# Loading one input block earlier, regrouping three small copies, and swapping the last two matmul groups in a hand-ordered state-space and MLP kernel

## Chip, cores and metric

The kernel runs on one core of a Trainium2 chip. The metric is the device time of one execution in microseconds (us). A core has five engines that run their own instruction lists side by side and wait for each other by semaphores: TensorE (PE, matmuls into psum), VectorE (DVE), ScalarE (ACT), GpSimd (POOL) and SyncE (SP, which here only issues DMAs).

## What is computed

The input x has 2048 rows of 448 columns. It is normalized per row (xn), and two branches work on xn: a linear state-space recurrence over the rows, and an MLP behind a second normalization. The result is their gated product added to x. Cut to what matters:

```python
def _A_ref(x, ...):                       # state-space branch, 448 complex states
    Lam_bar = jnp.exp(dt * Lam)
    B_bar = ((Lam_bar - 1.0) / Lam)[:, None] * Bmat
    Bu = jnp.einsum("bld,pd->blp", x + 0j, B_bar)
    for t in range(L):                    # L = 2048
        h = Lam_bar[None, :] * h + Bu[:, t, :]
    return 2.0 * jnp.einsum("blp,dp->bld", hseq, Cmat).real + x * Dskip

def _B_ref(x, w1, b1, w2, b2):            # MLP, 448 -> 1792 -> 448
    h = _gelu(jnp.einsum("bsd,df->bsf", _layernorm(x), w1) + b1)
    return jnp.einsum("bsf,fd->bsd", h, w2) + b2

xn = _layernorm(x)
return x + _A_ref(xn, ...) * _silu(_B_ref(xn, ...))
```

## The kernel before

**Tiling.** The 2048 rows are eight blocks of 256 (x0 to x7). A block is two "parities" of 128 rows each, even rows and odd rows, because the recurrence is done two rows at a time. Two blocks make a group; there are four groups, g = 0 to 3. Matrices are kept with 128 partitions; 448 columns are 3 x 128 + 64, so w1 is stored as four slices of rows, of which the fourth (w1's last 64 rows and, as a 65th, the bias b1) fills only half of the partitions.

**Stages of a group.** Normalize (bn_stats L381, bn_aggr L385, then a reciprocal root, on POOL as L424 to L428, then the scaling, L450 on DVE or L451 on ACT), giving xn and xn2 (normalized twice); transpose both (DMA transposes, L89; for the first block PE transposes instead). Then

- `mm1`: xn2 times w1, then gelu. For group 0 in halves (`mm1_half`, matmuls L746, gelu L752), one block at a time; for the other groups with all 512 columns (L726, gelu L736). L726 uses the partition halves in two steps, `own` and `other`, and for this needs w1's last 64 rows a second time, in partitions 64 to 127 of the fourth slice. A unit of `mm1` covers two of the 14 column tiles of w1 and writes two psum banks; units go round the bank pairs (0,1), (2,3), (5,6).
- `mm2`: gelu's output times w2 (14 matmuls L760), plus b2 (DVE, L763, reads bank 5 or 6), silu (ACT, L764).
- `bu`: xn times the input matrix (L652, bank 4), copied out by ACT (L656); `ssm`: the scan over rows on DVE (L677) with its rotations before and after.
- `ym`: the states times the output matrices (L795, L798, L801), then on DVE the gate (L810) and the sum with x (L813, on DVE or POOL), then the store. `skip` (L776 on DVE, L775 on POOL) prepares the term with Dskip; in the last block it makes three steps, so that x + Dskip term times the gate is ready in `xr`.

**The second copy of w1's last rows.** Lines L848 to L854 make four copies, W0 to W3, one for each load chunk of w1 (512, 512, 512 and 256 columns). Each may run on ACT (L851) or DVE (L852). Every unit of `mm1` after group 0 (L726) waits for all four, because they write under one name, `w1b`; for the same reason each copy waits for the one before it.

**The last block.** Where the last `ym` (group 3, block 1) handles odd rows, it is split by columns into two parts, 0 to 256 and 256 to 448 (L824), each with its own psum bank, gate, sum and store; the even rows have one part of 448 columns. The store of the 256 columns is issued from ACT, the other two from SP (L822).

**Preparing the matrices.** While group 0 is in work, DVE and ACT build the recurrence's input matrix: `combine` multiplies one half (L590 on ACT or L591 on DVE, into one of two `tmp` buffers) and adds the other (L593 on DVE). Its seven results LB0 to LB6 are transposed by DMA into BT0 to BT6 for `bu`.

**The order.** All work is first recorded as tasks (a few instructions of one engine each, with what they read and write), in the order in which the Python code comes to them. `Plan.link` works out who depends on whom. Then `emit` writes the tasks out in the order of one long hand-kept list, `ORDER` (L161 to L180): an entry is a task's number or its name (W0 to W3, H.. for the first half of an `mm1` unit, D.., O.., B..). Each engine gets its tasks in that order and runs them strictly one after another; a task waits by semaphore for its dependencies on other engines and, where there is one, on its own. A second list, `SECOND` (L181 to L183), names tasks that take the other of two allowed engines. There is no scheduler at run time, and no code outside of the two lists decides the order.

Of the kernel before, what the change touches and what calls it, by code (L numbers as in the profile page):

```python
# [9 lines left out]
BF = dt.bfloat16  # L10
# [148 lines left out]


ORDER = [int(k) if k.isdigit() else k for k in """  # L161
ST 0 18 22 10 88 1 19 16 23 15 20 2 21 11 3 9 27 12 24 8 17 14 13 25 5 7 6 26 89 4 28 90 96 91 29 45 30 97 92 98 93 31 46 47 94 99 48 63 103
95 32 53 100 49 54 101 50 102 33 51 52 114 64 44 106 65 55 38 108 116 56 105 115 39 107 57 109 40 117 58 118 41 120 42 119 36 110 122 34 121
111 37 144 124 35 104 123 43 60 112 62 125 59 B0 126 DH 72 113 67 B1 296 68 69 128 B2 70 127 300 298 73 B3 151 130 129 299 191 148 132 303
131 149 297 134 133 301 302 150 304 136 152 135 142 155 138 66 156 143 153 140 154 137 157 271 139 71 146 308 305 74 165 76 75 141 306 61
309 145 79 307 166 268 82 272 163 BF 83 77 310 86 169 164 181 158 277 269 159 401 180 400 270 170 167 398 147 160 274 W0 405 168 404 W1 182
W2 399 W3 171 280 402 403 183 161 406 172 H10 173 275 162 H11 192 278 184 281 356 174 H12 175 357 185 358 311 78 410 360 80 176 81 H13 361
312 411 229 407 412 408 362 230 409 501 502 H15 363 500 314 188 231 359 315 504 383 189 506 503 H16 232 505 507 508 H14 186 368 178 364 369
187 233 509 365 179 512 366 234 H21 513 177 237 316 H20 367 238 460 313 239 458 510 461 235 242 190 246 373 243 459 245 514 195 193 196 511
236 247 H24 244 H23 194 199 251 466 85 197 200 84 464 198 203 87 249 252 201 253 240 202 241 205 248 204 317 370 206 215 262 217 207 382 318  # L170
218 257 216 258 319 208 254 259 250 D0 263 255 260 209 320 371 256 264 321 210 219 221 D1 220 211 223 265 266 273 222 376 267 413 374 322
224 212 225 D2 326 276 213 227 226 379 325 279 228 214 D3 327 282 331 465 333 323 283 414 285 375 377 332 380 H26 415 334 467 H22 O00 335
470 324 484 462 471 328 289 330 284 416 339 329 286 340 463 261 341 342 H30 290 343 344 417 337 336 292 515 548 418 O01 345 H25 351 516 346
549 H31 485 347 287 348 468 288 293 349 H33 350 550 372 352 338 554 419 378 353 518 354 294 384 291 420 295 421 469 385 387 422 551 423 517
O10 555 388 574 391 389 424 519 428 386 427 475 392 429 437 394 435 425 520 472 426 390 430 436 431 521 432 476 473 481 522 438 O11 433 381
523 440 395 482 447 393 478 434 448 524 575 439 441 442 443 449 450 453 444 451 445 525 446 355 479 452 H32 526 454 H34 455 552 396 556 553
456 397 529 457 H36 557 H35 530 560 531 558 561 539 527 538 559 486 565 483 474 528 487 536 477 535 489 480 534 532 562 537 541 O20 566 533
540 493 488 542 563 544 567 490 564 568 491 494 492 543 545 496 569 546 571 570 O21 495 547 581 572 497 573 578 498 576 O30 499 577 582 593
579 585 583 594 595 580 596 589 584 586 587 590 588 591 592
""".split()]  # L180
SECOND = [int(k) if k.isdigit() else k for k in """  # L181
142 143 144 157 163 167 171 173 195 201 219 223 308 309 407 411 413 416 484 485 508 509 512 515 516 518 519 575 W0 W1 W2
""".split()]  # L183


# [743 lines left out]
```

## Time and profile before

| what | value |
|---|---|
| median of three runs | 155.3 us (155.3 to 155.35) |
| the profiled execution's own time | 155.38 us |
| its span, first to last instruction | 153.6 us |
| granted TensorE clock | 0.997 |
| busy share of PE, DVE, ACT, POOL | 97%, 80%, 72%, 22% |
| HBM read, written | 6.20 MB, 1.84 MB |

How to read the profile's rows. A row of the timeline gives the start in us from the beginning of the span, the duration in us, the engine, the line of the kernel, the operation, the tile that it writes and those that it reads (numbers left out, so that w1_sb and w2_sb both read `w_sb`, and xn_sb and xn2_sb both `xn_sb`), the shape, and how many instructions were merged into the row; in brackets stands how long the engine stood idle before it and what ended that. PEld is PE's loading of weights, which runs beside its matmuls; SPq and ACTq are the issuing of DMAs by these engines. The ends of matmuls are modelled. Instructions of DVE and ACT overlap a little: one that waits for nothing starts somewhat before the end of the one before it. A row of the DMA view gives the tile, the issuing engine, how many DMAs, their size, and the us from issue to landing.

### The profile page before, as it was taken

How to read it: one execution, taken by the hardware profiler on the slowest of the kernel's cores; microseconds unless marked ns; L12 is line 12 of the kernel's file. 1: busy time of each engine (PE TensorE's matmuls, PEld its weight loads, DVE VectorE, ACT ScalarE, POOL GpSimd, SP SyncE). 2: the span in 40 equal slices, each digit the busy share in tenths (PEclk: the TensorE clock that was granted, in tenths of full speed). 3: DMA queues.
4: the chain of work that ended last, by engine and by line, in shares of the span. 5: the costliest groups of instructions: out<-in, count | busy, mean ns of one | idle time of the engine just before them, and what ended most of it. 6: DMA issues, size and time to landing. Idle time of an engine off the chain costs nothing.

```text
span 153.6 us, 2968 instructions
## 1 busy us (share of the span) xinstructions
PE 148.8 (97%) x1055; PEld 88.1 (57%) x1055; DVE 122.8 (80%) x263; ACT 110.8 (72%) x190; POOL 34.2 (22%) x114
## 2 busy tenths in 40 slices
PE   7999999999999999999999999999999999999991
PEld 2689955445564555665544456755666455555560
DVE  5686989998967999899898864494986972999564
ACT  3867769899959988699999999832294889661100
POOL 6466491074000050310003310210006000000230
PEclk9999999999999999999999999999999999999998
DMA  4999976989996870000020121121300100001013
GB/s 94 282 316 399 263 178 125 154 157 179 223 141 110 153 137 0 0 4 0 2 46 18 38 82 64 21 38 27 94 4 0 60 0 0 4 0 62 0 66 113
DMA packets 31512, 14.04 MB, mean 91 GB/s; under 512 B 25733, under 2 KB 31113, under 8 KB 31498
## 3 DMA queue, kind: packets, MB, share of 16 engines
q1 hardware_dynamic: 31344, 13.79, 39.5%
q8 instruction: 8, 0.13, 0.3%
q10 hardware_dynamic: 154, 0.07, 0.2%
q14 instruction: 6, 0.05, 0.1%
HBM read 6.20 MB, written 1.84 MB: 52 GB/s over the span
## 4 chain that ended last, share of the span: by engine, by line
PE 80%; ACT 5%; DVE 4%; DMA 3%; POOL 3%; SPq 2%; issue 1%; ACTq 0%; DVEq 0%
PE psum L726 22%; PE psum L760 21%; PE psum L652 14%; PE psum L795 13%; PE psum L798 4%; DMA w_sb<-in_B_w_dram 3%; PE psum L631 3%; PE psum L746 2%; SPq L90 2%; ACT xn_sb L451 1%; DVE lnst L381 1%; POOL lnw L426 1%; ACT WT L574 1%; PE psum L801 1%; ACT L576 1%
## 5 line engine op out<-in xcount | busy, mean ns | idle before, releaser
L760 PE MATMUL psum<-w_sb,gT 128*128 128x448 bf16 x224 | 44.5, 353 | 0.0
L726 PE MATMUL psum<-xn2T,w_sb 64*128 64x512 bf16 x294 | 33.7, 378 | 0.2 <-ACT w_sb L851 0.2
L760 PEld LDWEIGHTS psum<-w_sb,gT 128*128 128x128 bf16 x224 | 21.8, 98 | 19.5 <-issue 0.2
L736 ACT ACTIVATE gT<-psum,b1f 128x512 bf16<-128x512 f32 x42 | 25.9, 690 | 3.2 <-PE psum L726 3.1
L726 PEld LDWEIGHTS psum<-xn2T,w_sb 64*128 64x128 bf16 x294 | 15.6, 109 | 16.8 <-issue 2.3
L652 PE MATMUL psum<-xnT,BT 128*128 128x256 bf16 x196 | 24.1, 273 | 0.0
L652 PEld LDWEIGHTS psum<-xnT,BT 128*128 128x128 bf16 x196 | 18.5, 98 | 6.4 <-issue 3.1
L677 DVE TENSOR_TENSOR_SCAN s_f<-cw,cur,v_sb 128x256 f32<-128x256 f32 x21 | 15.1, 740 | 0.2
L451 ACT ACTIVATE xn_sb<-x_all,lnw 128x448 bf16<-128x448 bf16 (+1 forms) x21 | 13.4, 668 | 1.3 <-POOL lnw L428 1.2
L764 ACT ACTIVATE g_sb<-o 128x448 bf16<-128x448 f32 x16 | 8.9, 572 | 6.4 <-DVE o L763 6.2
L746 PE MATMUL psum<-xn2T,w_sb 128*128 128x256 bf16 x112 | 12.9, 273 | 0.4 <-issue 0.3
L746 PEld LDWEIGHTS psum<-xn2T,w_sb 128*128 128x128 bf16 x112 | 11.8, 111 | 1.2 <-issue 0.6
L795 PE MATMUL psum<-CZ,h_sb 128*128 128x448 bf16 x56 | 11.9, 353 | 0.0
L810 DVE TENSOR_TENSOR t<-psum,g_sb 128x448 bf16<-128x448 f32 (+2 forms) x10 | 5.7, 575 | 7.4 <-ACT g_sb L764 3.7
L656 ACT ACTIVATE u_sb<-psum 128x512 bf16<-128x512 f32 x12 | 7.1, 593 | 5.8 <-PE psum L652 5.8
L763 DVE TENSOR_TENSOR o<-psum,b2bc 128x448 f32<-128x448 f32 x16 | 9.6, 613 | 1.5 <-PE psum L760 1.5
L795 PE MATMUL psum<-CQ,h_sb 128*128 128x448 bf16 (+2 forms) x54 | 10.6, 332 | 0.0
L752 ACT ACTIVATE gT<-psum 128x512 bf16<-128x512 f32 x14 | 8.2, 590 | 3.3 <-PE psum L746 3.2
L381 DVE BATCH_NORM_STATS2 lnst<-x_all 128x6 f32<-128x448 bf16 x14 | 8.3, 612 | 1.2 <-DMA x_all<-in_A_x_dram 1.1
L590 ACT ACTIVATE tmp<-Cr,cw 128x448 f32<-128x448 bf16 (+1 forms) x12 | 7.9, 672 | 1.0 <-DVE CQ L593 0.9
L691 POOL TENSOR_TENSOR cwk<-s_f,ang 128x3 f32<-128x3 f32 x3 | 1.1, 352 | 32.6 <-DVE s_f L677 32.5
L795 PEld LDWEIGHTS psum<-CZ,h_sb 128*128 128x128 bf16 x56 | 5.4, 98 | 4.7 <-issue 0.4
(156 smaller groups left out, 211.9 us busy)
## 6 DMA issues: line engine op xcount, KB each, us to landing
out_dram<-tmp SPq DMA_DIRECT2D x7, 224.0 KB, 2.0
x_all<-in_A_x_dram SPq DMA_DIRECT2D x3, 448.0 KB, 4.7
w_sb<-in_B_w_dram SPq DMA_DIRECT2D x3, 448.0 KB, 7.0
w_sb<-in_B_w_dram SPq DMA_DIRECT2D x3, 384.0 KB, 5.2
Bn<-in_A_B_im_dram SPq DMA_DIRECT2D x1, 336.0 KB, 9.1
Bn<-in_A_B_re_dram SPq DMA_DIRECT2D x1, 336.0 KB, 9.6
x_all<-in_A_x_dram SPq DMA_DIRECT2D x2, 112.0 KB, 2.1
x_all<-in_A_x_dram SPq DMA_DIRECT2D x1, 224.0 KB, 4.4
```

Of the source, the lines that this page charges most:

```text
L381: dve([lambda e, b=b, par=par, q=q: e.bn_stats(lnst[:, q, :], x_all[:, 2 * g + b, par, :])], [f"x{2 * g + b}"] + (["xmT0p1"] if (g, b) == ...
L451: ("act", [lambda e, o=o, i=i: e.activation(o, i, ACT.Identity, bias=nb, scale=rs) for o, i in pairs], 0.75, 0.2)]
L652: fns = [lambda e, r=r, m=m, d=d: e.matmul(psum[:, 4, r * NK:(r + 1) * NK], BT[:, m, d, :], xnT[:, gx, d, :], start=(d == 0), stop=(d == 6 ...
L677: dve(lambda e, i=i, ri=ri, init=init: e.tensor_tensor_scan(s_f[:, i, ri, :], col(R2, i).to_broadcast([128, NK]), v_sb[:, i, ri, :], init, ...
L726: return lambda e: e.matmul(psum[:, b0 + k, :], w1_sb[halves[h], d, fcol(2 * j + k)], rhs[halves[h], d, :, :], start=first and d == 0, sto ...
L736: act([lambda e, k=k: e.activation(gT[:, gb, 2 * j + k, :], psum[:, b0 + k, :], ACT.Gelu_apprx_tanh, bias=b1f[:, 2 * j + k:2 * j + k + 1]) ...
L746: fns = [lambda e, k=k, d=d: e.matmul(psum[:, banks[k], :].rearrange("p (r c) -> p r c", r=2)[:, :, cs], w1_sb[:, d, fcol(2 * j + k)], rhs ...
L752: act(lambda e: e.activation(gT[:, 0, 2 * j:2 * j + 2, :].rearrange("p k (r c) -> p k r c", r=2)[:, :, :, cs], psum[:, b0:b0 + 2, :].rearr ...
L760: fns = [lambda e, fi=fi: e.matmul(psum[:, bk, 0:D], gT[:, gb, fi, q * 128:(q + 1) * 128], w2_sb[:, fi, :], start=(fi == 0), stop=(fi == N ...
L763: dve(lambda e: e.tensor_tensor(o2[:, ob, :], psum[:, bk, 0:D], b2bc[:], ALU.add), [f"ps{bk}", "b2bc"], [f"oo{ob}"], 0.62, prio - 76)
L764: act(lambda e: e.activation(g_sb[:, gs, :], o2[:, ob, :], ACT.Silu), [f"oo{ob}"] + (["silu"] if g == 0 else []), [f"g{gs}"], 0.58, prio - ...
L795: fns = [lambda e, k=k: e.matmul(psum[:, bk, c0:c1], h_sb[:, hb, k, k0:k0 + 128], cm[:, k, c0:c1], start=(k == 0), stop=False) for k in ra ...
```

## The change

Only the two lists change. No task is added, removed or altered.

1. SP issues the load of x1 (task 26) directly behind the two loads of x0, ahead of both loads of w1's first chunk (24 and 25: `w1_0` and its last rows `w1r_0`). Before, it came behind them.
2. On DVE the copies W0, W1, W2 come sooner behind each other. Before, three other tasks of DVE stood between W0 and W1 (405, 168, 404: an aggregate, the add LB1, an aggregate) and none between W1 and W2; the add LB4 (170) stood ahead of W0. Afterwards a bn_stats and an aggregate (401, 402) stand between W0 and W1, LB4 between W1 and W2, and LB1 and the other aggregates behind W2. Ahead of them, the add LB0 (164) now stands before the multiplication 169 (L591) instead of behind it. On ACT the multiplication 167 (L590) comes one table (L574) and one silu earlier.
3. Behind the copies: the L763 of task 275 now comes ahead of LB2 (172); LB5 (174) comes behind both instructions of LB6's multiplication (175), LB6 (176) and an L776 (281); one scaling of xn (311) goes from DVE to ACT, and another (312) comes behind three bn_stats. On SP the transpose of xnT0_1 (147) comes ahead of BT3 and BT0 (181, 180), and the load of x6 and x7 (192) ahead of BT1 and BT4 (182, 183). On POOL one small product (78) comes ahead of the reciprocal root of group 2 (406).
4. In the last block PE multiplies the 448 columns of the even rows (585) ahead of the 192 columns of the odd rows (593); before it was the other way round. The 256 columns (589) stay last. The sum of the 192 columns (595) goes from DVE to POOL, and the last step of `skip` (577) from POOL to DVE. The store of the 192 columns (596) is issued behind the other two of SP. In the stretch before, DVE's order changes a little: the L763 of task 569 comes ahead of the sum 545 (L707), and a sum (495, L813) comes later.

The two lists, cut to the places that the steps above name (the numbers around them are the same or are moved by one or two places):

```diff
 ORDER
-ST 0 18 22 10 88 1 19 16 23 15 20 2 21 11 3 9 27 12 24 8 17 14 13 25 5 7 6 26 89 4 28 ...
+ST 0 18 22 10 88 1 19 23 16 20 15 2 21 11 3 9 27 12 26 8 17 14 13 24 5 89 7 6 25 90 4 28 ...
...
-166 268 82 272 163 BF 83 77 310 86 169 164 181 158 277 269 159 401 180 400 270 170 167 398 147 160 274 W0 405 168 404 W1 182
-W2 399 W3 171 280 402 403 183 161 406 172 H10 173 275 162 H11 192 278 184 281 356 174 H12 175 357 185 358 311 78 410 360 80 176 81 H13 361
-312 411 229 407 412 408 362 230 409 501 502 ...
+268 166 79 272 82 163 BF 83 310 77 86 164 78 169 147 277 158 269 400 167 181 159 398 W0 401 270 402 W1 180 274 170 160 W2 405 168
+W3 404 399 192 182 171 161 403 280 406 173 H10 275 183 162 172 H11 278 356 175 184 H12 357 176 358 80 410 281 174 360 185 81 H13 361 411 407
+229 412 311 408 362 501 230 H15 502 409 363 500 231 312 ...
...
-497 578 498 576 O30 499 577 582 593
-579 585 583 594 595 580 596 589 584 586 587 590 588 591 592
+498 578 576 O30 499 582 583 579 577
+580 584 585 593 589 586 594 595 587 588 590 591 596 592
 SECOND
-... 223 308 309 407 ... 519 575 W0 W1 W2
+... 223 308 309 311 407 ... 519 575 577 W0 W1 W2 595
```

More of the change, by code (lines that the diff above doesn't have):

```diff
@@ L161 @@
 ORDER = [int(k) if k.isdigit() else k for k in """
[L162 to L165, printed above, removed]
@@ L166 @@
-309 145 79 307 166 268 82 272 163 BF 83 77 310 86 169 164 181 158 277 269 159 401 180 400 270 170 167 398 147 160 274 W0 405 168 404 W1 182
-W2 399 W3 171 280 402 403 183 161 406 172 H10 173 275 162 H11 192 278 184 281 356 174 H12 175 357 185 358 311 78 410 360 80 176 81 H13 361
-312 411 229 407 412 408 362 230 409 501 502 H15 363 500 314 188 231 359 315 504 383 189 506 503 H16 232 505 507 508 H14 186 368 178 364 369
-187 233 509 365 179 512 366 234 H21 513 177 237 316 H20 367 238 460 313 239 458 510 461 235 242 190 246 373 243 459 245 514 195 193 196 511
@@ L170 @@
[L170 to L177, printed above, removed]
@@ L178 @@
-540 493 488 542 563 544 567 490 564 568 491 494 492 543 545 496 569 546 571 570 O21 495 547 581 572 497 573 578 498 576 O30 499 577 582 593
-579 585 583 594 595 580 596 589 584 586 587 590 588 591 592
+ST 0 18 22 10 88 1 19 23 16 20 15 2 21 11 3 9 27 12 26 8 17 14 13 24 5 89 7 6 25 90 4 28 91 96 29 45 97 92 98 30 93 46 47 99 94 48 63 103 31
+95 53 100 49 54 32 101 50 102 51 33 106 52 114 64 44 65 108 55 105 116 38 56 115 107 109 39 118 57 117 58 40 120 41 119 110 42 122 121 111
+36 144 124 34 123 37 112 104 125 35 126 60 113 43 62 59 296 DH 72 B0 128 67 127 68 300 B1 298 69 70 130 B2 151 73 129 299 B3 148 132 191 131
@@ new lines @@
+303 149 297 134 133 301 302 150 304 136 152 135 155 142 138 66 156 143 153 140 154 137 157 271 139 71 308 305 74 146 165 76 141 306 75 309
+145 61 307 268 166 79 272 82 163 BF 83 310 77 86 164 78 169 147 277 158 269 400 167 181 159 398 W0 401 270 402 W1 180 274 170 160 W2 405 168
+W3 404 399 192 182 171 161 403 280 406 173 H10 275 183 162 172 H11 278 356 175 184 H12 357 176 358 80 410 281 174 360 185 81 H13 361 411 407
+229 412 311 408 362 501 230 H15 502 409 363 500 231 312 314 188 359 315 504 383 506 H16 503 232 189 505 507 508 H14 186 368 364 369 178 233
@@ new lines @@
+187 509 365 512 179 366 234 H21 513 237 177 H20 316 238 367 460 239 458 510 313 235 242 461 190 373 246 243 459 514 245 195 193 196 511 236
+H24 247 244 H23 199 194 251 466 200 85 197 464 84 203 198 87 317 249 252 201 253 240 202 370 241 205 248 204 206 215 262 217 207 318 382 218
+257 216 319 258 208 254 250 259 D0 263 255 209 371 320 260 256 264 321 210 219 221 D1 220 211 223 265 266 273 222 376 267 413 374 224 322
+212 225 D2 326 213 276 227 226 379 325 279 228 214 D3 327 282 331 465 333 323 283 414 285 377 375 332 380 H26 415 334 H22 467 O00 335 470
@@ new lines @@
+324 484 462 289 471 328 330 284 416 339 329 340 286 261 463 341 H30 290 342 343 417 344 292 336 337 548 515 418 O01 H25 351 345 516 346 H31
+485 549 347 287 348 468 288 293 349 350 H33 550 352 372 554 338 419 378 353 518 354 294 384 420 291 295 421 469 385 387 422 551 423 517 O10
+555 388 574 391 389 424 519 428 386 475 427 392 429 437 394 435 425 520 472 426 390 430 436 431 521 432 476 473 481 522 438 O11 433 381 440
+523 395 482 393 447 434 478 448 524 575 439 441 442 443 449 450 444 453 451 525 479 445 446 355 452 H32 526 454 H34 455 552 396 456 556 397
@@ L180 @@
+553 529 457 H36 530 557 H35 531 560 558 539 561 527 538 559 486 565 483 474 528 487 536 477 535 489 480 534 532 562 537 O20 541 566 533 540
+493 488 542 563 544 567 490 564 568 491 494 492 543 496 569 545 570 571 546 547 O21 497 581 572 495 573 498 578 576 O30 499 582 583 579 577
+580 584 585 593 589 586 594 595 587 588 590 591 596 592
 """.split()]
 SECOND = [int(k) if k.isdigit() else k for k in """
-142 143 144 157 163 167 171 173 195 201 219 223 308 309 407 411 413 416 484 485 508 509 512 515 516 518 519 575 W0 W1 W2
+142 143 144 157 163 167 171 173 195 201 219 223 308 309 311 407 411 413 416 484 485 508 509 512 515 516 518 519 575 577 W0 W1 W2 595
```

## The prediction

> **What bounds the kernel now.** I read the page first, then the chain that ended last, then engine by engine the stretches in which the diff moves something. The profiled execution took 155.38 us; its span is 153.6 us, so 1.78 us lie around it. The median of the three runs is 155.3 us. The sum below is made against 155.38 and lowered by 0.08 us at the end. About 0.2% (0.31 us) is what a measurement of this kernel can tell from no change.
>
> ```profile
> span 153.6 us, 2968 instructions
> PE 148.8 (97%) x1055; PEld 88.1 (57%) x1055; DVE 122.8 (80%) x263; ACT 110.8 (72%) x190; POOL 34.2 (22%) x114
> ```
>
> TensorE (PE) is busy 97% of the span, and the diff adds or takes away no matmul. So only three things can change the time: when PE begins, where it waits, and what remains after its last matmul. The end of the chain shows the last of these:
>
> ```profile
> 148.90 0.77 PE psum L798 x4
> 149.76 0.63 DVE t L810
> 150.42 0.39 DVE tmp L813
> 150.81 0.35 DVE t L810
> 151.18 0.42 DVE tmp L813
> ```
>
> PE ends its 448 columns at 149.67, and then VectorE (DVE) has four instructions to do: L810 and L813 on these columns, then on the 256 that PE does last. The other two places, PE's begin and a stop in mid-kernel, stand below with their parts.
>
> **Part 1, x1 ahead of w1.** SP issues x1 where w1's first chunk was, and that chunk's two loads one place (0.57 us) later. Nothing behind them moves.
>
> ```profile
> 1.71 1.05 SPq L90 DMA_DIRECT2D w_sb<-in_B_w_dram  x2
> 2.81 0.57 SPq L90 DMA_DIRECT2D x_all<-in_A_x_dram  x1
> w_sb<-in_B_w_dram SPq DMA_DIRECT2D x1, 384.0 KB, 3.6
> x_all<-in_A_x_dram SPq DMA_DIRECT2D x1, 224.0 KB, 4.4
> 6.84 1.67 PEld L746 LDWEIGHTS psum<-xn2T,w_sb 128*128 128x128 bf16 x16 [0.42 <-issue]
> 8.90 1.13 PEld L746 LDWEIGHTS psum<-xn2T,w_sb 128*128 128x128 bf16 x11 [0.39 <-DMA w_sb<-in_B_w_dram]
> 7.24 0.63 DVE L381 BATCH_NORM_STATS2 lnst<-x_all 128x6 f32<-128x448 bf16 x1 [0.47 <-DMA x_all<-in_A_x_dram]
> ```
>
> In these rows the first chunk lands at 1.71 + 3.6 = 5.3 us, its small rest (the second of the x2) right behind, while PE first uses them at 6.84: over 1 us of cover. x1 landed last of the three, at 2.81 + 4.4 = 7.2. Afterwards the rest of w1's chunk is the last of the same bytes. If it needs w1's 3.6 us from an issue at 2.81, it lands at 6.4; if it takes x1's 4.4, at 7.2. Both cost nothing, or almost: PE goes through the chunk's 16 loads and then stands still for 0.39 us at 8.90 until the second chunk is there, so a start up to some 0.3 us late is taken out of that wait. The bytes ahead of the second chunk are the same, so I leave its landing at 8.9. DVE's 0.47 us wait for x1 goes, but what it feeds is not late now (PE's transposes of that block come behind six units of matmuls), so that is worth nothing. I take **0**, with ends of -0.3 (the second chunk lands earlier and its whole wait goes) and +0.3 (the first chunk lands 0.6 us behind the 6.84).
>
> The Trainium skill (DMA: Bandwidth & Descriptors, section Queues, rings and completion order) says that each DMA engine consumes descriptors in ring order. By it, x1's bytes stand in front of w1's, and the first chunk can only be later; the rows agree in that x1, issued last, landed last. That speaks against this part, but here it has some 1 us of cover.
>
> **Part 2, the copies of w1's last rows (W0 to W3).** All matmuls of L726 wait for all four, three on DVE (L852) and the last on ACT (L851), which waits for the third.
>
> ```profile
> 24.08 0.61 DVE L763 TENSOR_TENSOR o<-psum,b2bc 128x448 f32<-128x448 f32 x1
> 24.61 0.44 DVE L591 TENSOR_SCALAR tmp<-Bn,cw 128x448 f32<-128x448 bf16 x1
> 24.97 0.68 DVE L593 SCALAR_TENSOR_TENSOR Bn<-Bn,cw,tmp 128x448 bf16<-128x448 bf16 x1
> ...
> 28.39 0.29 DVE L852 COPY w_sb<-w_sb 64x512 bf16<-64x512 bf16 x1
> 28.71 0.18 DVE L385 BATCH_NORM_AGGREGATE lnmv<-lnst 128x2 f32<-128x6 f32 x1
> 28.93 0.68 DVE L593 SCALAR_TENSOR_TENSOR Bn<-Bn,cw,tmp 128x448 bf16<-128x448 bf16 x1
> ...
> 29.74 0.61 DVE L852 COPY w_sb<-w_sb 64x512 bf16<-64x512 bf16 x2
> ...
> 31.59 0.69 DVE L593 SCALAR_TENSOR_TENSOR Bn<-Bn,cw,tmp 128x448 bf16<-128x448 bf16 x1
> 32.19 1.15 DVE L763 TENSOR_TENSOR o<-psum,b2bc 128x448 f32<-128x448 f32 x2
> ```
> ```profile
> 24.19 0.65 ACT L590 ACTIVATE tmp<-Bn,cw 128x448 f32<-128x448 bf16 x1
> 28.25 0.65 ACT L590 ACTIVATE tmp<-Bn,cw 128x448 f32<-128x448 bf16 x1
> 30.45 0.41 ACT L851 ACTIVATE w_sb<-w_sb 64x256 bf16<-64x256 bf16 x1 [0.51 <-DVE w_sb L852]
> 30.91 5.77 PE L726 MATMUL psum<-xn2T,w_sb 64*128 64x512 bf16 x50 [0.18 <-ACT w_sb L851]
> ```
>
> Now: the third copy ends at 30.35, ACT's at 30.86, and PE begins at 30.91 after 0.18 us of standing still. In the new order one L593 (0.60 from start to start) and one L385 (0.20) fall behind the third copy, but another L593 is moved ahead of an L591 and must wait for ACT's L590 until 24.84; it starts at 24.89 instead of taking its turn at 24.61. So the third copy ends at about 30.35 - 0.80 + 0.28 = 29.8 to 29.9 and ACT's at about 30.3. **PE's stop at 30.91 goes**: it can start when its own earlier matmuls allow, about 0.3 us sooner.
>
> What is late next? L726's third unit, 2.5 us on, writes the psum banks that the two L763 of 32.19 read. Among those who waited for L763 stands:
>
> ```profile
>   PEld psum L726: 0.4, 1
> ```
>
> That pair ends at 32.19 + 1.15 = 33.34, and PE waits for it 0.4 us (its weight loads) already. Between 24.08 and the end of that pair DVE has the same instructions in both orders, so only its gaps count. An instruction that waits for nothing starts 0.08 us before the last one's end (24.61 against 24.69); one at a copy's side, or one that waits, starts 0.03 behind (28.71 against 28.68): 0.11 apart. The wait for ACT at 24.89 costs 0.28. Two waits go: the L593 of 28.93 came 0.03 behind ACT's L590 (28.25 + 0.65), which now runs earlier: 0.11; and that of 31.59 stood 0.13 idle, and one of the L763 now comes ahead of it: 0.21. Two more held starts around the copies, which stand apart on DVE (two other instructions between the first and second, one between the second and third) cost 0.22. Sum: 0.28 - 0.11 - 0.21 + 0.22 = **+0.18 us** for the pair. PE's third unit starts so much later than before, though its first started 0.3 us sooner: the stop is moved and grows. I take **+0.15** for this part, since the gaps are only good to some hundredths. Ends: +0.3 if neither wait of DVE goes, and -0.15, which the next part sets.
>
> The Trainium skill (VectorE: DVE Perf Modes, section Two Vector instructions with no wait between them) says that an instruction whose output starts in another quadrant of partitions than the last one's is held until all earlier ones are done. The 0.03 behind each L852, which reads partitions from 0 and writes from 64, agrees; by that rule copies that truly stood together would save held starts, and by the new order they do not.
>
> **Part 3, what else moves near there.** One scaling of xn (L450 on DVE) goes to ACT as an L451, ahead of the pair of 37.74.
>
> ```profile
> 37.74 1.09 ACT L451 ACTIVATE xn_sb<-x_all,lnw 128x448 bf16<-128x448 bf16 x2
> 38.74 0.57 ACT L656 ACTIVATE u_sb<-psum 128x512 bf16<-128x512 f32 x1
> 39.89 0.50 PE L652 MATMUL psum<-xnT,BT 128*128 128x256 bf16 x3
> BT<-Bn SPq DMA_TRANSPOSE x7, 4.4
> ```
>
> A single 448-column form of it takes about 0.66 from start to start (the pair's 1.09 is a 448- and a 64-column form; bounds 0.55 and 0.75). ACT gets to it about 0.1 us sooner than now, so L656 ends not at 39.31 but at about 39.7, and PE's next L652 (39.89 now, 40.04 with part 2) still finds it done: nothing. Had PE kept the 0.3 us, it would wait here until about 39.75: this is why part 2 cannot gain more than 0.15. SP's transposes change places (xnT0_1 ahead of BT3 and BT0, the last x load ahead of BT1 and BT4); BT4's input comes about 1.8 us later on DVE (its L593 moves behind the second copy, to about 29.5), BT5's about 1.9, to 36. Issued from SP at about 32 and 36.5 and with 4.4 us to landing they are there by 37 and 41; their users on PE begin at 39.89 and, two groups of L726 later, beyond 43. ACT's and SP's later queue slips by about half a microsecond and is hidden by the same margins. After that PE runs without a gap to the end, and DVE and ACT take their work from it, so the +0.15 is carried through.
>
> **Part 4, the last block.** PE's last groups change from 192, 448, 256 columns to 448, 192, 256. PE ends at the same moment, with the 256 group.
>
> ```profile
> 150.15 0.27 PE L801 MATMUL psum<-CQ,h_sb 128*128 128x256 bf16 x1
> 144.17 0.61 DVE L810 TENSOR_TENSOR t<-xr,g_sb 128x448 bf16<-128x448 f32 x1
> 145.78 0.80 DVE L810 TENSOR_TENSOR t<-xr,g_sb 128x448 bf16<-128x448 f32 x1
> 150.73 0.42 DVE L810 TENSOR_TENSOR t<-psum,g_sb 128x256 bf16<-128x256 f32 x1
> 145.01 1.09 POOL L775 TENSOR_TENSOR xr<-xd,g_sb 128x448 f32<-128x448 bf16 x1 [23.33 <-ACT g_sb L764]
> ```
>
> PE is done at 150.42, but DVE's L810 on the 256 starts only at 150.73, behind the 448's two instructions: 0.31 late. In the new order the 448 group is done on PE one 192 group earlier, 149.67 - 0.58 = 149.09. DVE then does its L810 (0.63) to 149.76, the 192's L810 (under the 256's 0.42) to 150.1 and the 448's add (0.39) to 150.4, and is free when PE ends: L810 on the 256 at 150.46, its add (0.42) to 151.33 instead of 151.18 + 0.42 = 151.60. The 192's add goes to POOL: by the 448-column row (1.09) it takes 0.5, if all of that is per column, to 0.7, from 150.2 to about 150.8, and its store goes out from SP at once, ahead of the last one from ACT. The second L775, which also adds x, goes from POOL to DVE, at 147.66 to 148.3, where DVE stood idle. So the last store starts 0.27 sooner: **-0.27**, or -0.15 if POOL's add and DVE's last add get in each other's way. I take -0.22.
>
> The Trainium skill (SBUF — State Buffer, section Who interferes with whom) says that a DVE instruction with two SBUF inputs and a GpSimd one that reads SBUF block each other. The L810 of 145.78, 0.80 us beside POOL's L775 where its like took 0.61 us at 144.17, agrees. By that rule POOL's new add can hold up DVE's last add until it ends, here until about 150.9: a loss of at most 0.05 by my times.
>
> **Sum:** 155.38 + 0 + 0.15 + 0 - 0.22 = 155.31, less 0.08 for the median: 155.23, that is **155.2 us**. Its own range, from 0.1 either way on parts 2 and 4, is 155.0 to 155.4.
>
> **The rivals.**
> (a) *The first loads run better.* With all of w1 in a row the second chunk lands at 8.6 or sooner, and the 0.39 us wait goes: -0.3, so 154.9. For it: x1 between the chunks took 4.4 us for half the bytes of the first chunk, which took 3.6. Against it: the bytes are the same. Chance 0.26.
> (b) *Slower: the psum read-out on DVE.* The place is L726's third unit; the price is the time by which the L763 pair ends behind 33.34. It decides from about +0.5, that is if the held starts, the wait for ACT and a later L590 add up and neither old wait goes; with a tail gain of 0.15 that makes 155.6 to 155.7. Chance 0.14.
> (c) *Slower: the first chunk lands too late,* behind 7.2, so that the wait at 8.90 cannot take it up: with 0.5 us late, 155.6. For it: x1's 4.4 us. Chance 0.10.
> (d) *The change does not do what it says:* the copies are still apart, PE's stop only moves, and POOL's add takes the tail's gain: 155.3 to 155.45. Chance 0.12.
> My forecast has the remaining 0.38.
>
> **Chances and range.** Faster by over 0.2% (below 155.0): (a) and the low end of the forecast, 0.34. Slower by over 0.2% (above 155.6): most of (b) and (c), 0.18. Within: 0.48. The range 154.75 to 155.65 takes in (a), and (b) and (c) to their beginning.
>
> **What would show it.** In the profile after: the first load of L746 at 6.8 and the wait at 8.90 still there (part 1); no wait of L726 for L851, but one for L763 at about 33.5, and the second L652 group at about 40.0 (part 2); L656 done by 39.8 (part 3); the L810 on 256 columns starting within 0.1 us of PE's last matmul (part 4). It is wrong if PE starts L746 later than 7.2, if it starts its L726 unit on the read-out banks earlier than 33.3, or if the last add waits for POOL.

## The result: 155.19 us, faster by 0.27%

| | before | after |
|---|---|---|
| median of 20 runs each (lowest to highest) | 155.4 us (155.12 to 156.54) | 155.19 us (154.59 to 155.52) |
| ratio after / before | | 0.9973, 95% interval 0.996 to 0.9986 |
| profiled execution / its span | 155.38 / 153.6 us | 155.14 / 153.4 us |

The time lies where it was forecast (155.2). By the medians the gain is 0.21 us (0.14%), by the ratio 0.42 (0.27%); the ratio lies close to that of the means, which differ by 0.41. The forecast had 0.07. So the likeliest class, "within 0.2%" (0.48), fits the medians, while the ratio is just beyond it, on the faster side (0.34).

The first lines of the page of after:

```profile
span 153.4 us, 2972 instructions
PE 148.5 (97%) x1055; PEld 87.7 (57%) x1055; DVE 122.7 (80%) x262; ACT 111.1 (72%) x191; POOL 34.8 (23%) x114
```

The waits of PE in after (us in total, times, longest):

```profile
PE psum L837 <- DVE still L294: 1.0, 1, 1.0
PE psum L726 <- DVE o L763: 0.4, 1, 0.4
PE psum L746 <- DMA w_sb<-in_B_w_dram: 0.3, 1, 0.3
PE psum L746 <- DVE xn2T L407: 0.2, 1, 0.2
```

In the second row L726 waits for L763, the read-out; among PE's waits no row is left for the copy L851, for which it stood still in before. The L837 row is in every kernel here.

The start, by the weight loads of L746 in the timeline of after:

```profile
6.41 1.67 PEld L746 LDWEIGHTS psum<-xn2T,w_sb 128*128 128x128 bf16 x16 [0.41 <-DVE xn2T L407]
8.67 1.68 PEld L746 LDWEIGHTS psum<-xn2T,w_sb 128*128 128x128 bf16 x16 [0.59 <-DMA w_sb<-in_B_w_dram]
10.58 1.68 PEld L746 LDWEIGHTS psum<-xn2T,w_sb 128*128 128x128 bf16 x16 [0.23 <-issue]
```

x1 among the DMA issues of its page:

```profile
x_all<-in_A_x_dram SPq DMA_DIRECT2D x1, 224.0 KB, 2.7
```

x1 lands in 2.7 us (4.4 before; 2.6 to 3.0 in the nine profiles here with x1 ahead, 3.8 to 4.4 in the five with it behind), and w1's first chunk is in time for a start 0.43 us earlier than before. The wait for the second chunk is still there and takes up half of that: its loads begin at 8.67 (8.90 before). Most of the rest goes in the stop of 0.23 us at 10.58, which before doesn't show. Block 1's first L746 matmul starts at 13.79 (13.86 before): 0.07 us sooner, in these two executions.

The middle, in the timeline of after. DVE:

```profile
24.87 0.68 DVE L593 SCALAR_TENSOR_TENSOR Bn<-Bn,cw,tmp 128x448 bf16<-128x448 bf16 x1 [0.27 <-ACT tmp L590]
...
28.41 0.17 DVE L385 BATCH_NORM_AGGREGATE lnmv<-lnst 128x2 f32<-128x6 f32 x1
28.60 0.29 DVE L852 COPY w_sb<-w_sb 64x512 bf16<-64x512 bf16 x1
...
29.64 0.29 DVE L852 COPY w_sb<-w_sb 64x512 bf16<-64x512 bf16 x1
...
31.44 0.36 DVE L776 TENSOR_TENSOR xd<-xn_sb,dbc 128x448 bf16<-128x448 bf16 x1
31.72 0.62 DVE L763 TENSOR_TENSOR o<-psum,b2bc 128x448 f32<-128x448 f32 x1
32.25 0.68 DVE L593 SCALAR_TENSOR_TENSOR Bn<-Bn,cw,tmp 128x448 bf16<-128x448 bf16 x1
32.84 0.62 DVE L763 TENSOR_TENSOR o<-psum,b2bc 128x448 f32<-128x448 f32 x1
```

ACT in the same timeline:

```profile
30.02 0.41 ACT L851 ACTIVATE w_sb<-w_sb 64x256 bf16<-64x256 bf16 x1 [0.30 <-DVE w_sb L852]
...
39.09 0.58 ACT L656 ACTIVATE u_sb<-psum 128x512 bf16<-128x512 f32 x1
```

PE there:

```profile
30.60 2.57 PE L726 MATMUL psum<-xn2T,w_sb 64*128 64x512 bf16 x22
33.52 3.21 PE L726 MATMUL psum<-xn2T,w_sb 64*128 64x512 bf16 x28 [0.36 <-DVE o L763]
...
39.94 1.70 PE L652 MATMUL psum<-xnT,BT 128*128 128x256 bf16 x14
```

The copies are ready 0.4 us sooner (ACT's ends at 30.43, 30.86 before), so L726 begins at 30.60 instead of 30.91. But its third unit waits for the second L763, which ends at 33.46 (33.34 before), and begins at 33.52. Between the two L763 stands an L593.

The end of the chain of after:

```profile
150.35 0.12 PE psum L801
150.48 0.03 issue
150.50 0.43 DVE t L810
150.94 0.02 issue
150.96 0.43 DVE tmp L813
```

DVE and POOL just ahead of that, in its timeline:

```profile
149.26 0.89 DVE L810 TENSOR_TENSOR t<-psum,g_sb 128x448 bf16<-128x448 f32 x2 [0.72 <-PE psum L798]
150.06 0.38 DVE L813 TENSOR_TENSOR tmp<-t,x_all 128x448 bf16<-128x448 bf16 x1
150.22 0.63 POOL L813 TENSOR_TENSOR tmp<-t,xr 128x192 bf16<-128x192 bf16 x1 [4.14 <-DVE t L810]
```

Two DVE instructions now begin behind the end of PE's last matmul, not three (before also had the 448 columns' add there, at 150.42). PE's last matmul ends at 150.46, the last add at 151.39: 0.93 us, against 1.18 in before.

One measure serves all that follows: the **distance** from block 1's first L746 matmul to the end of the last add. It is 151.60 - 13.86 = 137.74 us in before and 151.39 - 13.79 = 137.6 in after, and in the three pairs of kernels that differ only in x1's place it agrees to 0.01 us. It is not always that exact: tail_only below, which has before's order up to the last stretch, reaches its first L726 unit 0.06 us sooner than before does. What lies ahead of the distance varies more: over the fourteen profiles, one of each kernel, that matmul starts between 13.50 and 14.04.

### The profile page after: what moved, and what is told of

It reads as the page before. It is cut to its first block, busy times and chain, and to the rows that moved or that the text cites. A ratio compares the mean times of both kernels' runs of the same rounds, so it can differ in the third digit from the quotient of the medians.

```text
span 153.4 us, 2972 instructions
## 1 busy us (share of the span) xinstructions
PE 148.5 (97%) x1055; PEld 87.7 (57%) x1055; DVE 122.7 (80%) x262; ACT 111.1 (72%) x191; POOL 34.8 (23%) x114
## 2 busy tenths in 40 slices
DMA packets 31512, 14.04 MB, mean 92 GB/s; under 512 B 25733, under 2 KB 31113, under 8 KB 31498
## 3 DMA queue, kind: packets, MB, share of 16 engines
q1 hardware_dynamic: 31344, 13.79, 41.5%
## 4 chain that ended last, share of the span: by engine, by line
PE 76%; SPq 9%; DVE 6%; DMA 5%; issue 1%; ACT 1%; POOL 0%; POOLq 0%; DVEq 0%
PE psum L760 21%; PE psum L726 20%; PE psum L652 14%; PE psum L795 13%; SPq L90 9%; DMA b1b<-in_B_b_dram 5%; PE psum L798 4%; PE psum L631 3%; DVE Bn L593 2%; DVE o L763 1%; DVE lnst L381 1%; PE psum L801 1%; ACT xn_sb L451 1%; DVE w_sb L852 1%; PE psum L636 1%
## 5 line engine op out<-in xcount | busy, mean ns | idle before, releaser
L726 PE MATMUL psum<-xn2T,w_sb 64*128 64x512 bf16 x294 | 33.7, 378 | 0.4 <-DVE o L763 0.4
L726 PEld LDWEIGHTS psum<-xn2T,w_sb 64*128 64x128 bf16 x294 | 15.6, 109 | 16.9 <-issue 2.3
L652 PE MATMUL psum<-xnT,BT 128*128 128x256 bf16 x196 | 24.1, 273 | 0.0
L652 PEld LDWEIGHTS psum<-xnT,BT 128*128 128x128 bf16 x196 | 18.6, 98 | 6.4 <-issue 2.9
L451 ACT ACTIVATE xn_sb<-x_all,lnw 128x448 bf16<-128x448 bf16 (+1 forms) x22 | 14.0, 672 | 1.2 <-POOL lnw L428 1.2
L746 PE MATMUL psum<-xn2T,w_sb 128*128 128x256 bf16 x112 | 13.1, 273 | 0.6 <-DMA w_sb<-in_B_w_dram 0.3
L746 PEld LDWEIGHTS psum<-xn2T,w_sb 128*128 128x128 bf16 x112 | 11.7, 112 | 1.6 <-DMA w_sb<-in_B_w_dram 0.6
L656 ACT ACTIVATE u_sb<-psum 128x512 bf16<-128x512 f32 x12 | 7.1, 595 | 5.8 <-PE psum L652 5.8
L810 DVE TENSOR_TENSOR t<-psum,g_sb 128x448 bf16<-128x448 f32 (+2 forms) x10 | 5.7, 574 | 7.0 <-ACT g_sb L764 3.7
L763 DVE TENSOR_TENSOR o<-psum,b2bc 128x448 f32<-128x448 f32 x16 | 9.7, 614 | 1.0 <-PE psum L760 1.0
L590 ACT ACTIVATE tmp<-Cr,cw 128x448 f32<-128x448 bf16 (+1 forms) x12 | 7.9, 671 | 0.9 <-DVE CQ L593 0.5
```

Of the source, the lines that this page charges most:

```text
L451: ("act", [lambda e, o=o, i=i: e.activation(o, i, ACT.Identity, bias=nb, scale=rs) for o, i in pairs], 0.75, 0.2)]
L652: fns = [lambda e, r=r, m=m, d=d: e.matmul(psum[:, 4, r * NK:(r + 1) * NK], BT[:, m, d, :], xnT[:, gx, d, :], start=(d == 0), stop=(d == 6 ...
L726: return lambda e: e.matmul(psum[:, b0 + k, :], w1_sb[halves[h], d, fcol(2 * j + k)], rhs[halves[h], d, :, :], start=first and d == 0, sto ...
L746: fns = [lambda e, k=k, d=d: e.matmul(psum[:, banks[k], :].rearrange("p (r c) -> p r c", r=2)[:, :, cs], w1_sb[:, d, fcol(2 * j + k)], rhs ...
L763: dve(lambda e: e.tensor_tensor(o2[:, ob, :], psum[:, bk, 0:D], b2bc[:], ALU.add), [f"ps{bk}", "b2bc"], [f"oo{ob}"], 0.62, prio - 76)
```

## Experiments

**The theory:** after is three changes that don't touch each other: the tail brings -0.27, the middle costs 0.12 (one stop of PE replaced by another, in front of the third L726 unit), the first loads bring next to nothing. **The rivals:** the first loads bring the gain and the rest is noise; in the middle, it isn't the read-out that is late but something behind it (L656, or gelu), so that mending the read-out brings nothing; in the tail, PE's order brings the gain and not POOL's add.

| kernel | what it is | median, us | ratio to before (95%) | distance, us |
|---|---|---|---|---|
| x1_only | before + x1 ahead | 155.27 | 0.9971 (0.9942 to 0.9999) | 137.73 |
| mid_only | before + the change's middle | 155.48 | 0.9998 (0.9971 to 1.0025) | 137.87 |
| tail_only | before + the change's last block | 155.09 | 0.9958 (0.9929 to 0.9988) | 137.42 |
| x1_back | after, x1 behind w1's chunk | 155.45 | 1.0004 (0.9972 to 1.0037) | 137.60 |
| readout_first | after, the L763 pair first | 155.1 | 0.9971 (0.9955 to 0.9987) | 137.60 |
| readout_xn | + one L451 back to L450 | 154.67 | 0.9949 (0.9936 to 0.9963) | 137.41 |
| readout_xn_bu | + L652 ahead of L726's fourth unit | 154.72 | 0.9954 (0.9939 to 0.997) | 137.31 |
| lb0_back | after, L591 ahead of LB0 again | 154.63 | 0.9951 (0.9933 to 0.9968) | 137.25 |
| copies_together | after, three copies in a row | 154.98 | 0.9966 (0.9951 to 0.9981) | 137.33 |
| tail_no_pool | after, the 192's sum on DVE | 155.13 | 0.9984 (0.9972 to 0.9997) | 137.84 |
| all_three | readout_xn + lb0_back | 154.65 | 0.9938 (0.9918 to 0.9957) | 137.04 |
| all_three_x1_back | all_three, x1 behind w1's chunk | 154.87 | 0.9986 (0.9959 to 1.0013) | 137.05 |

The medians are of 5 to 12 executions each. The first four and the last four ran in two sessions on one chip (before there 155.42 and 155.36), the four between on another (155.5); a ratio is to before in the same session.

### Taking the change apart

**x1_only**, before with step 1 alone:

```diff
-12 24 8 17 14 13 25 5 7 6 26 ...
+12 26 8 17 14 13 24 5 89 7 6 25 ...
```

> The kernel before with x1's load ahead of w1's first chunk and nothing else changed. Theory (the gain comes from the last block): within 0.1 us of before, since PE starts L746 sooner (about 6.4 instead of 6.85) but then waits for the second and third chunk of w1 and passes the third at about 10.6 instead of 10.7. Rival (the gain comes from the first loads): 0.2 us or more faster, with L746's later units at least 0.2 us sooner.

The trace gives a distance like that of before. The median is 0.15 us lower, between what theory and rival said, and the interval ends at 1.

**mid_only**, after without steps 1 and 4:

```diff
-12 26 8 17 14 13 24 5 89 7 6 25 ...
+12 8 17 14 13 24 5 89 7 6 25 26 ...
...
-580 584 585 593 589 586 594 595 587 588 590 591 596 592
+593 585 589 594 595 580 586 587 590 591 596 584 588 592
 SECOND
-... 575 577 W0 W1 W2 595
+... 575 W0 W1 W2
```

> The kernel before with the regrouped copies and all that is moved in mid-kernel, x1 and the last block as before. Theory: 0.1 us slower (0.0 to 0.2): PE's stop in front of L726's first unit goes, and one of about 0.4 us stands in front of its third, for L763. Rival (the copies bring the gain): 0.15 us or more faster.

The distance grows by 0.13 us, with the stop for L763 in the place of that for L851. The interval of the times holds no change as well as twice that: the trace shows this term, the measured times don't.

**tail_only**, before with step 4 alone and the stretch ahead of it as changed.

```diff
-593 585 589 594 595 580 586 587 590 591 596 584 588 592
+580 584 585 593 589 586 594 595 587 588 590 591 596 592
 SECOND
-... 575 W0 W1 W2
+... 575 577 W0 W1 W2 595
```

> The kernel before with the last block as changed (448 columns ahead of the 192, the 192's sum on POOL, the x step of skip on DVE). Theory: 0.25 us faster, the last add ending 0.9 us behind PE's last matmul instead of 1.2. Rivals: no gain (POOL's sum blocks DVE's last add, or the store of the 192 columns comes last).

From PE's last matmul to the end of the last add it takes 0.92 us instead of 1.19: -0.27, as the rows of the prediction gave it. The medians say -0.33, and the distance -0.32, since PE's last matmul too came 0.05 sooner.

**x1_back**, after without step 1.

```diff
-12 26 8 17 14 13 24 5 89 7 6 25 ...
+12 8 17 14 13 24 5 89 7 6 25 26 ...
```

> The changed kernel with x1's load put back behind w1's first chunk. Theory: the sum of the other two parts, +0.1 and -0.25, so about 0.15 us faster than before and within 0.1 us of the changed kernel. Rival (the gain comes from the first loads): no faster than before.

From block 1's first matmul on it is after, to 0.01 us. So by the trace x1's place is worth what it shifts that matmul, and that shift is drowned: x1_back's profiled execution (155.04) is faster than that of after, its median 0.26 us slower. By the measured times the rival's sign came, no faster than before, though the interval (0.9972 to 1.0037) also holds the 0.15 us of the theory.

### What the middle waits for

**readout_first**: the L763 pair without the L776 (280) and the LB2 (172) ahead of it and in it.

```diff
-W3 404 399 192 182 171 161 403 280 406 173 H10 275 183 162 172 H11 278 356 ...
+W3 404 399 192 182 171 161 403 406 173 H10 275 183 162 H11 278 280 172 356 ...
```

> The changed kernel with the second pair of L763 (the read-out of psum banks 5 and 6) put directly behind the last aggregate on DVE, ahead of L776 and L593. Theory (L726's third unit waits for that pair): PE's stop in front of the third unit goes (it starts 2.4 us behind the first, not 2.9), and the next bound is the gelu pair of ACT at about 35.45, so the first L652 group starts some 0.2 us sooner than in the changed kernel: about 0.2 us faster than it. Rival (the stop is only read there, something else holds PE): the first L652 group starts at the same time from the start of block 1's matmuls.

The stop at the third unit is gone, and the first L652 group comes 0.2 us sooner. The second doesn't: its distance from block 1's first matmul is 26.15 us (26.14 in after), and the 0.2 us that was expected at the end did not come (137.60, as in after). ACT in the timeline of readout_first:

```profile
37.71 1.73 ACT L451 ACTIVATE xn_sb<-x_all,lnw 128x448 bf16<-128x448 bf16 x3
39.34 0.58 ACT L656 ACTIVATE u_sb<-psum 128x512 bf16<-128x512 f32 x1
```

PE there:

```profile
30.71 4.72 PE L726 MATMUL psum<-xn2T,w_sb 64*128 64x512 bf16 x42
35.61 1.05 PE L726 MATMUL psum<-xn2T,w_sb 64*128 64x512 bf16 x8 [0.17 <-ACT gT L736]
...
38.23 1.70 PE L726 MATMUL psum<-xn2T,w_sb 64*128 64x512 bf16 x14
40.06 1.69 PE L652 MATMUL psum<-xnT,BT 128*128 128x256 bf16 x14
```

The second L652 group begins 0.13 us behind the end of the L726 (39.93) instead of 0.06 ahead of it as in after, and 0.14 behind the end of L656 (39.92), which stands on ACT behind three L451. Three, since the change gave ACT one more. The next kernel takes it away.

**readout_xn**: as readout_first, and the scaling 311 on DVE again, there ahead of 312.

```diff
-229 412 311 408 362 501 230 H15 502 409 363 500 231 312 ...
+229 412 408 362 501 230 H15 502 409 363 500 311 231 312 ...
 SECOND
-... 308 309 311 407 ...
+... 308 309 407 ...
```

> As readout_first, and the xn scaling that the change gave to ACT is back on DVE, behind the three bn_stats. Theory: the same as readout_first to within 0.1 us, since the gelu pair and not L656 is the bound; L656 ends 0.6 us sooner. Rival (the scaling on ACT holds L656 and so PE's second L652 group): 0.2 us faster than readout_first.

I expected no more than 0.1 us over readout_first and was wrong; the rival was right: distance 137.41, 0.19 sooner, all of it at the second L652 group. ACT in its timeline:

```profile
37.47 1.09 ACT L451 ACTIVATE xn_sb<-x_all,lnw 128x448 bf16<-128x448 bf16 x2
38.46 0.58 ACT L656 ACTIVATE u_sb<-psum 128x512 bf16<-128x512 f32 x1
```

PE there:

```profile
39.48 1.70 PE L652 MATMUL psum<-xnT,BT 128*128 128x256 bf16 x14
```

L656 ends at 39.04, well ahead of the second L652 group, which no longer waits. That shows L656 as the bound behind the read-out.

**readout_xn_bu**: as readout_xn, with PE doing the first L652 group (229) ahead of L726's fourth unit (H13), which had waited for gelu.

```diff
-... 185 81 H13 361 411 407
-229 412 ...
+... 185 81 361 411 407 229
+H13 412 ...
```

> As readout_xn, and PE does the first L652 group ahead of the L726 unit that waits for ACT's gelu pair. Theory: no stop is left between L726's first unit and the second L652 group, which starts 0.45 to 0.55 us sooner than in the changed kernel; 0.5 us faster than it, 0.7 us faster than before. Rival (a later stop takes the gain back, on DVE, ACT or a DMA): PE's end moves less than its second L652 group.

Missed: the second L652 group comes 0.29 us sooner than in after, not 0.45 to 0.55, and the distance is 0.28 us shorter. The wait for gelu went, but another came. Among its weight loads' waits stands one which none of the other kernels here has:

```profile
PEld psum L726 <- PE psum L726: 0.5, 1, 0.5
```

PE in its timeline:

```profile
36.59 2.82 PE L726 MATMUL psum<-xn2T,w_sb 64*128 64x512 bf16 x22
39.35 1.70 PE L652 MATMUL psum<-xnT,BT 128*128 128x256 bf16 x14
```

The first 14 of these 22 matmuls are the two halves (8 and 6) of one unit, on the same two psum banks. They now stand directly behind each other, and the second half waits by semaphore for the first half's last matmul. In after 22 matmuls of L726 took 2.57 us (30.60); here 2.82, so that the order cost 0.25.

**lb0_back**: after with one pair of step 2 turned back, the multiplication 169 ahead of LB0 (164).

```diff
-... 77 86 164 78 169 147 ...
+... 77 86 78 169 164 147 ...
```

> The changed kernel with LB0's L593 back behind the L591, so that it no longer waits for ACT's L590. Theory (gaps on DVE set the stop): the second L763 pair ends 0.25 us sooner, PE's third unit of L726 starts that much sooner, and after the gelu pair's bound some 0.2 us are left at the first L652 group. Rival (held starts around the copies alone make the stop): no change.

Distance 0.34 us shorter than that of after: more than expected. The wait for ACT goes. It cost DVE more than the 0.27 us of its bracket: in after the L593 starts at 24.87, where its turn would have been 24.52 (0.53 behind the L763 of 23.99, as in before). The L763 pair ends sooner, and so do ACT's L590 and the tables behind it, which DVE's adds had made late; so gelu does not become the next bound here, as it does in readout_first. This one exchange costs more than the whole middle does on balance (0.12).

**copies_together**: the three copies truly behind each other.

```diff
-... W0 401 270 402 W1 180 274 170 160 W2 405 168
+... W0 270 W1 180 274 160 W2 401 402 170 405 168
```

> The changed kernel with W0, W1 and W2 directly behind each other on DVE. Theory (each start beside a copy is held until the one before it has ended, 0.11 us each): two such starts fewer, so the second L763 pair ends 0.2 us sooner and L726's third unit starts 0.2 us sooner; ACT's gelu pair then allows the first L652 group some 0.2 us sooner. Rival (the spaces between copies cost nothing): the pair ends at the same time from L726's first unit.

DVE in its timeline:

```profile
27.78 0.93 DVE L852 COPY w_sb<-w_sb 64x512 bf16<-64x512 bf16 x3
```

The three are done at 28.71 (29.93 in after). L726's first unit does not begin sooner for it. But the third does, by 0.27 us, as the distance shows too (-0.26): ahead of the read-out DVE has two starts fewer that come behind the end of the instruction before, worth some 0.2 by the 0.11 of the expectation. So putting copies together helps, by a way other than their being ready earlier, and after does not put them together.

### The tail without POOL

**tail_no_pool**: after with the 192's sum (595) on DVE and the last step of skip (577) on POOL, PE's order as changed.

```diff
 SECOND
-... 575 577 W0 W1 W2 595
+... 575 W0 W1 W2
```

> The changed kernel with the same order on PE, but the 192 columns' sum back on DVE, ahead of the 448's, and the x step of skip back on POOL. Theory: DVE is late again when PE ends, by 0.2 us, so the last add ends 1.1 us behind PE's last matmul (0.93 in the changed kernel, 1.19 before). Rival (the order on PE alone brings the gain): 0.93 again.

Its POOL and DVE in the timeline:

```profile
146.20 1.30 POOL L775 TENSOR_TENSOR xr<-x_all,xr 128x448 f32<-128x448 bf16 x1
146.64 1.11 DVE L813 TENSOR_TENSOR tmp<-t,x_all 128x448 bf16<-128x448 bf16 x1
...
149.29 0.89 DVE L810 TENSOR_TENSOR t<-psum,g_sb 128x448 bf16<-128x448 f32 x2 [0.58 <-PE psum L798]
150.22 0.36 DVE L813 TENSOR_TENSOR tmp<-t,xr 128x192 bf16<-128x192 bf16 x1
150.49 0.38 DVE L813 TENSOR_TENSOR tmp<-t,x_all 128x448 bf16<-128x448 bf16 x1
150.79 0.42 DVE L810 TENSOR_TENSOR t<-psum,g_sb 128x256 bf16<-128x256 f32 x1
151.24 0.42 DVE L813 TENSOR_TENSOR tmp<-t,xr 128x256 bf16<-128x256 bf16 x1
```

The 192's sum stands in front of the last L810, which begins at 150.79, 0.30 behind PE's end (150.22 + 0.27), as in before. From PE's end to the end of the last add it takes 1.17 us (1.18 in before, 0.93 in after). So PE's new order brings nothing by itself. The sum's move to POOL would not either, by two rows of before, though no run has it alone:

```profile
148.44 0.36 DVE L813 TENSOR_TENSOR tmp<-t,xr 128x192 bf16<-128x192 bf16 x1
149.76 0.62 DVE L810 TENSOR_TENSOR t<-psum,g_sb 128x448 bf16<-128x448 f32 x1 [0.66 <-PE psum L798]
```

There the 192's sum was done before DVE stood idle, so taking it away would have freed nothing. The gain needs both: the order brings the 448's pair forward, and POOL takes the one instruction that then stands in its way.

### All at once

**all_three**: lb0_back and readout_xn in one kernel, x1 ahead. Against after:

```diff
-... 77 86 164 78 169 147 ...
+... 77 86 78 169 164 147 ...
-W3 404 399 192 182 171 161 403 280 406 173 H10 275 183 162 172 H11 278 356 ...
+W3 404 399 192 182 171 161 403 406 173 H10 275 183 162 H11 278 280 172 356 ...
-229 412 311 408 362 501 230 H15 502 409 363 500 231 312 ...
+229 412 408 362 501 230 H15 502 409 363 500 311 231 312 ...
 SECOND
-... 308 309 311 407 ...
+... 308 309 407 ...
```

> The changed kernel with LB0 back behind the L591, the second L763 pair directly behind the last aggregate, and the xn scaling back on DVE. Theory: no stop between L726's first unit and the second L652 group, which starts 8.8 us behind that unit (9.34 in the changed kernel); PE ends 0.5 us sooner from block 1's first matmul on, so 0.5 us faster than the changed kernel and 0.7 us faster than before. Rival (something behind it takes the gain back): PE's end moves by less than its second L652 group.

PE in its timeline:

```profile
30.83 5.59 PE L726 MATMUL psum<-xn2T,w_sb 64*128 64x512 bf16 x50
36.35 1.70 PE L652 MATMUL psum<-xnT,BT 128*128 128x256 bf16 x14
37.98 1.70 PE L726 MATMUL psum<-xn2T,w_sb 64*128 64x512 bf16 x14
39.62 1.70 PE L652 MATMUL psum<-xnT,BT 128*128 128x256 bf16 x14
```

From the first L726 unit to the second L652 group no bracket is left in PE's rows. The distance is 0.55 us shorter than that of after, and shorter than that of each of the two kernels that it joins. The median is 154.65, 0.71 us below that of before, as expected; the ratio's interval (0.9918 to 0.9957) overlaps with theirs.

**all_three_x1_back**: the same with x1 behind w1's chunk.

```diff
-12 26 8 17 14 13 24 5 89 7 6 25 ...
+12 8 17 14 13 24 5 89 7 6 25 26 ...
```

> As all_three, with x1's load back behind w1's first chunk. Theory (x1's place is worth nothing): the same time as all_three to within 0.15 us, and the same distance from block 1's first matmul to the end. Rival (x1 ahead lets w1's second chunk land sooner): L746's third unit starts 0.2 us later and so does everything behind it.

The same distance, and in the two profiles the same start (14.04 and 14.03) although PE began later here. Its weight loads in the timeline:

```profile
7.33 3.75 PEld L746 LDWEIGHTS psum<-xn2T,w_sb 128*128 128x128 bf16 x35 [0.47 <-issue]
```

Those of all_three:

```profile
6.89 1.67 PEld L746 LDWEIGHTS psum<-xn2T,w_sb 128*128 128x128 bf16 x16 [0.76 <-DVE xn2T L407]
9.01 2.05 PEld L746 LDWEIGHTS psum<-xn2T,w_sb 128*128 128x128 bf16 x19 [0.45 <-DMA w_sb<-in_B_w_dram]
```

A start 0.44 us later cost nothing here: it came out of the wait for the second chunk. Still the median is 0.22 us higher, more than the 0.15 that was expected at most.

## Why the prediction was right, and where it was not

**Part 1 (0; ends -0.3 and +0.3): its mechanism holds in the traces, its size is open.** The first chunk came in time (3.6 to 4.0 us from its issue in all fourteen profiles, x1 ahead or behind), the second set the pace (8.67, forecast 8.9). The two profiles give -0.07. All three pairs of kernels that differ only in x1's place lean towards x1 ahead in their medians, by 0.15 (155.27 against before's 155.42), 0.26 (155.19 against 155.45, in two sessions) and 0.22 (154.65 against 154.87), and by their ratios, 0.9973 against 1.0004 and 0.9938 against 0.9986 in the last two. The first interval ends at 1, those of the second pair overlap, those of the third just don't (0.9957, 0.9959). The traces show nothing beyond the spread of the start. The nine profiles with x1 ahead have block 1's first matmul at 13.79 on the mean, the five with it behind at 13.91. So 0 may be 0.1 to 0.2 too high. The single times show one thing more: of the 146 executions with x1 behind w1's chunk, 13 took 0.8 us or more above their kernel's median (155.78 to 157.23 us), of the 88 with x1 ahead none. No such execution was profiled. So it stays open whether x1's place does this, and by which transfer; one profile of a kernel can't tell it.

**Part 2 (+0.15): right, measured +0.12.** Each step came: LB0 at 24.87 (24.89 forecast), the third copy's end at 29.93 (29.8 to 29.9), ACT's at 30.43 (30.3), the end of the read-out at 33.46 (33.52), which from block 1's first matmul on is 0.19 later than in before, forecast 0.18. Inside that sum two sizes were off and cancelled, which is luck: LB0's wait cost 0.35 (0.34 by lb0_back) and not 0.28, so the other terms together gave back some 0.15 and not 0.10. Of the 0.19 the fourth unit gave 0.07 back: it had waited for gelu in before. The held starts are real. In after the copy of 28.60 starts 0.02 behind the end of the aggregate, where an instruction that waits for nothing starts 0.08 ahead; copies_together, with two fewer, is 0.26 faster. The rule of the Trainium skill on held starts (VectorE: DVE Perf Modes, Two Vector instructions with no wait between them) agrees; these rows give 0.1 us for each.

**Part 3 (nothing): right.** L656 ends at 39.67 (39.7 forecast). That PE, once given the 0.3 us, would wait there was said, and readout_first shows it (40.06), readout_xn that it is the extra L451.

**Part 4 (-0.22, from -0.27 by rows): the rows were right,** at -0.27 (tail_only; -0.25 by the rows of after). The 0.05 kept back for DVE and POOL in each other's way was not spent: POOL's add took 0.63 us (0.5 to 0.7 forecast) and ended at 150.85, before DVE's last add began at 150.96, which took 0.43, as in before. tail_no_pool shows that PE's order without the sum's move to POOL brings nothing.

**The sum.** By the traces -0.07 + 0.12 - 0.27 = -0.22 us; the profiled executions differ by 0.24, the medians by 0.21, the ratio's interval says 0.22 to 0.62. The forecast's 0.07 was short by 0.03 in part 2, 0.05 in part 4 and 0.07 or more in part 1. All three lean to one side. That the time came out at 155.2 all the same is in part luck: before itself had 155.4 in this measurement, and 155.3 in the three runs from which the forecast started. Rival (a) had the direction but not the place: the wait for the second chunk did not go. Rivals (b) and (c) did not come, nor did (d): PE's stop did only move, but the tail's gain stayed.

## What to carry to other kernels

A stop of the engine that is busy all the time is worth no more than the distance to the next late input: list who is late second and third (here copy, read-out, L656, gelu) before an earlier copy is paid for with a later read-out. Where an engine runs strictly in order, ask of each instruction ahead of a psum read-out whether anybody waits for it. Moving an L776 and an add behind it, exchanging two instructions and giving one scaling back to DVE shortened the distance by 0.55 us, more than the whole change does. At the end of a kernel, count the instructions between the last matmul and the last store, and give what isn't last to an idle engine; here the order of the matmuls alone gave nothing.

## What the runs showed of the hardware that was not expected

- L726's second half directly behind its first, on whose last matmul it waits by semaphore, cost 0.25 us in readout_xn_bu (2.82 against 2.57 us for 22 matmuls). In the other kernels other matmuls stand between them, and no such wait is listed.
- DVE's L813, with two SBUF inputs, took 1.11 us beside POOL's L775 (146.20 to 147.50) in tail_no_pool, 0.38 to 0.39 in the other rows shown. The rule on interference (the Trainium skill, SBUF — State Buffer, Who interferes with whom) agrees. The price is far larger than the 0.80 against 0.61 us that the trace of before showed.
- The first 14 us vary by 0.54 us over the nine profiles in which x1 is ahead and the first loads have the same order (13.50 to 14.03), while the 137 us after them agree to 0.01 us in the pairs that differ only in x1's place. An order of the first loads can't be judged by one profile; a difference of 0.1 us or more behind them can.
